# Moving the per-tile VectorE work of a two-layer gated FFN between the blocks of its matmul stream

## The chip, the cores and the metric

The kernel runs on one core of one Trainium2 chip. The metric is the device time in microseconds (us) of one execution. The engines are named as in the profile: PE is TensorE (its weight loads are a separate row, PEld), DVE is VectorE, ACT is ScalarE, POOL is GpSimd, SP is SyncE, which issues most DMAs (114 of the 118 issues in the profile of the kernel before; the other four are POOL's). A run is fast or slow; all comparisons below use fast runs.

## The reference

Two layers, each a gate by a long convolution (A) and a GELU-gated FFN (B), on x of 2048 x 576:

```python
x = A_q
x = x + A(layernorm(x)); x = x + B(layernorm(x))
x = x + A(layernorm(x)); x = x + B(layernorm(x))

# A(q): y depends on k, v and the filters only, not on x
kv = shift_conv(k) * v
y  = irfft(rfft(kv) * rfft(ssm_k)) + kv * ssm_D
A(q) = q * y
# B(x), F = 4608
B(x) = (gelu(x @ w_gate) * (x @ w_up)) @ w_down
```

Because y does not depend on x, it is computed once, at the start.

## The kernel before

The convolution stage fills `y_sb`. Then come eight *units*: layer 0, chunks 0 to 3, then layer 1, chunks 0 to 3. A chunk is 512 rows, which is 4 tiles of 128 rows. A unit goes through 36 *blocks* f of 128 hidden columns. In a block PE does 10 gate/up matmuls (`pg`, `pu`) and 8 down matmuls (`acc`), ACT does the gelu (`ga`), and DVE does `hT = ga * pu`, which the down matmul needs. Between them lies per-tile work on DVE, which below is counted in *pieces*:

```python
def _gate_residual(...):            # one "gate" piece: x + layernorm(x) * y for one tile
    _ln_stats(...)                  # 2 bn_stats, bn_aggr, add eps on DVE; rstd (pow) on POOL
    nc.vector.scalar_tensor_tensor(out=t[:], in0=x_in_ap, scalar=mv[:, 0:1], in1=y_ap, ...)
    nc.vector.scalar_tensor_tensor(out=x_out_ap, in0=t[:], scalar=rstd[:, 0:1], in1=x_in_ap, ...)

def ln_transpose(c):                # for each of 4 tiles one "LN" piece, then the transposes
    for j in range(STC):
        _ln_stats(...)
        nc.vector.tensor_scalar(out=xn[:, 0:D], ...)          # normalised tile, bf16
        # ... 64 more columns of it
    for (c0, dst) in blocks:        # 6 PSUM tiles, 4 transposes each, on PE
        pt = psum_gu.tile([P, CH], BF16, tag="gu")
        # ... 4 x nc.tensor.transpose(pt <- xn)
        nc.vector.tensor_copy(out=dst, in_=pt[:])             # xnT, the rhs of gate/up

def epilogue(layer, c, acc):        # end of a unit
    for j in range(STC):
        # ... x_c (layer 0) or ob (layer 1) <- x_c + acc, two DVE instructions
    for j in range(STC):
        # ... layer 1: DMA out;   layer 0: _gate_residual(...) of the tile, for layer 1
```

The main loop:

```python
psum_gu = ctx.enter_context(tc.tile_pool(name="psum_gu", bufs=3, space=PSUM))
# ... loads of x; gate pieces and ln_transpose of chunk 0
for ui, (layer, c) in enumerate(units):
    # ...
    pgu = gate_up(0)
    for f in range(FT):                                   # FT = 36
        nxt = gate_up(f + 1) if f + 1 < FT else None
        hT = act_mul(*pgu)
        down(f, hT)
        pgu = nxt
        if f == min(6, FT - 1) and ui + 1 < len(units):   # next unit's chunk, in block 6
            nlayer, ncu = units[ui + 1]
            if ncu != c:
                if nlayer == 0:
                    gate_A1(ncu)                          # 4 gate pieces
                nxt_cur = ln_transpose(ncu)               # 4 LN pieces, 24 transposes
    epilogue(layer, c, acc)
```

The instructions of an engine do not run in the order of this text. In the trace of before, the four gates of chunk 1, written in block 6 of unit 0, run from 220.60 to 237.98 us, and the down matmuls of block 1 start only at 238.27. Where two compete, the one written first went first: the gates ahead of hT(0) (348.42 and 356.82 us).

Of the kernel before, what the change touches and what calls it, by code (L numbers as in the profile page):

```python
# [11 lines left out]
ALU = mybir.AluOpType  # L12
F32 = mybir.dt.float32
BF16 = mybir.dt.bfloat16
# [3 lines left out]
P = 128  # L18
# [218 lines left out]
def _ln_stats(nc, small, x_ap, D, eps_t, neghalf_t, mv_out, rstd_out, pfx):  # L237
    nchunk = 2 if D > nc.vector.BN_STATS_FMAX else 1
    w = D // nchunk
    stats = small.tile([P, nchunk, nc.vector.BN_STATS_DIM], F32, tag=pfx + "stats")  # L240
    for h in range(nchunk):
        nc.vector.bn_stats(out=stats[:, h, :], in_=x_ap[:, h * w:(h + 1) * w])  # L242
    nc.vector.bn_aggr(out=mv_out, in_=stats[:])
    ve = small.tile([P, 1], F32, tag=pfx + "ve")
    nc.vector.tensor_scalar_add(out=ve[:], in0=mv_out[:, 1:2], scalar1=eps_t[:, 0:1])  # L245
    nc.gpsimd.tensor_tensor(out=rstd_out, in0=ve[:], in1=neghalf_t[:, 0:1], op=ALU.pow)  # L246


def _gate_residual(nc, small, work, x_in_ap, y_ap, x_out_ap, D, eps_t, neghalf_t):
    mv = small.tile([P, 2], F32, tag="g_mv")  # L250
    rstd = small.tile([P, 1], F32, tag="g_rstd")
    _ln_stats(nc, small, x_in_ap, D, eps_t, neghalf_t, mv[:], rstd[:], "g_")
    t = work.tile([P, D], F32, tag="g_t", bufs=1)
    nc.vector.scalar_tensor_tensor(out=t[:], in0=x_in_ap, scalar=mv[:, 0:1], in1=y_ap,
                                   op0=ALU.subtract, op1=ALU.mult)
    nc.vector.scalar_tensor_tensor(out=x_out_ap, in0=t[:], scalar=rstd[:, 0:1], in1=x_in_ap,  # L256
                                   op0=ALU.mult, op1=ALU.add)
# [3 lines left out]
def ssm_geglu_kernel(ctx, tc, A_q, A_k, A_v, A_shift_k, A_ssm_k, A_ssm_D, B_x, B_w_gate, B_w_up,  # L261
                     B_w_down, out, debug=None):
    nc = tc.nc
    q2 = A_q[0]
    out2 = out[0]
    S, D = q2.shape
# [3 lines left out]
    NCH = S // CH  # L270
    STC = CH // P
    FT = F // P
# [56 lines left out]
    def xs(st):  # L329
        return x_c[st // STC][:, st % STC, :]  # L330

    def gate_A1(c):
        for j in range(STC):
            st = c * STC + j
            _gate_residual(nc, small, work, xs(st), y_sb[:, st, :], xs(st), D, eps_t, neghalf_t)

    psum_gu = ctx.enter_context(tc.tile_pool(name="psum_gu", bufs=3, space=PSUM))
    psum_acc = ctx.enter_context(tc.tile_pool(name="psum_acc", bufs=1, space=PSUM))
# [1 line left out]
    NLAYER = 2  # L340
    units = [(layer, c) for layer in range(NLAYER) for c in range(NCH)]

    def ln_transpose(c):
        xns = []
        for j in range(STC):
            st = c * STC + j
            mv = small.tile([P, 2], F32, tag="mv")
            rstd = small.tile([P, 1], F32, tag="rstd")
            _ln_stats(nc, small, xs(st), D, eps_t, neghalf_t, mv[:], rstd[:], "l_")
            xn = xnp.tile([P, XW], BF16, tag=f"xn{j}", bufs=1)  # L350
            nc.vector.tensor_scalar(out=xn[:, 0:D], in0=xs(st), scalar1=mv[:, 0:1],
                                    scalar2=rstd[:, 0:1], op0=ALU.subtract, op1=ALU.mult)
            if DREM:
                nc.gpsimd.memset(xn[:, D:D + DREM], 0.0)
                nc.vector.tensor_scalar(out=xn[:, D + DREM:XW], in0=xs(st)[:, D - DREM:D],
                                        scalar1=mv[:, 0:1], scalar2=rstd[:, 0:1],
                                        op0=ALU.subtract, op1=ALU.mult)
            xns.append(xn)
        xnT = xnp.tile([P, NDTF, CH], BF16, tag="xnT")
        xnT_rA = xnT_rB = None  # L360
        blocks = [(dt * P, xnT[:, dt, :]) for dt in range(NDTF)]
        if DREM:
            xnT_rA = xnp.tile([P, CH], BF16, tag="xnT_rA", name="xnT_rA")
            xnT_rB = xnp.tile([P, CH], BF16, tag="xnT_rB", name="xnT_rB")
            blocks.append((NDTF * P, xnT_rA[:]))
            blocks.append((NDTF * P + DREM, xnT_rB[:]))
        for (c0, dst) in blocks:
            pt = psum_gu.tile([P, CH], BF16, tag="gu")
            for j in range(STC):
                nc.tensor.transpose(out=pt[:, j * P:(j + 1) * P], in_=xns[j][:, c0:c0 + P], identity=ident[:])  # L370
            nc.vector.tensor_copy(out=dst, in_=pt[:])
        return xnT, xnT_rA, xnT_rB

    def epilogue(layer, c, acc):
        last_layer = layer == NLAYER - 1
        obs = []
        for j in range(STC):
            st = c * STC + j
            if last_layer:
                ob = work.tile([P, D], BF16, tag="pd_bf", bufs=3)  # L380
                obs.append(ob)
                dst_ap = lambda lo, hi: ob[:, lo:hi]
            else:
                dst_ap = lambda lo, hi: xs(st)[:, lo:hi]
            nc.vector.tensor_tensor(out=dst_ap(0, DM), in0=xs(st)[:, 0:DM], in1=acc[:, j, 0:DM], op=ALU.add)  # L385
            if DR:
                nc.vector.tensor_tensor(out=dst_ap(DM, D), in0=xs(st)[:, DM:D],
                                        in1=acc[:, STC, j * DR:(j + 1) * DR], op=ALU.add)
        for j in range(STC):
            st = c * STC + j  # L390
            if last_layer:
                eng = nc.sync
                eng.dma_start(out=out2[st * P:(st + 1) * P, :], in_=obs[j][:])
            else:
                _gate_residual(nc, small, work, xs(st), y_sb[:, st, :], xs(st), D, eps_t, neghalf_t)

    for c in range(NCH):
        nc.gpsimd.dma_start(out=x_c[c][:],
                            in_=q2[c * CH:(c + 1) * CH, :].rearrange("(st p) d -> p st d", p=P))
    gate_A1(0)  # L400
    wpool = ctx.enter_context(tc.tile_pool(name="weights", bufs=1))
    for g in range(1, NFG):
        alloc_w(wpool, g)
        load_w(g)
    cur = ln_transpose(units[0][1])
    for ui, (layer, c) in enumerate(units):
        xnT, xnT_rA, xnT_rB = cur
        acc = psum_acc.tile([P, STC + (1 if DR else 0), 512], F32, tag="acc")

        def gate_up(f):  # L410
            g, fi = divmod(f, FG)
            pg = psum_gu.tile([P, CH], F32, tag="gu")
            pu = psum_gu.tile([P, CH], F32, tag="gu")
            for (pd, wm, rr) in ((pg, wg[g], xnT_rA), (pu, wu[g], xnT_rB)):
                for dt in range(NDTF):
                    nc.tensor.matmul(pd[:], lhsT=wm[:, dt, fi * P:(fi + 1) * P], rhs=xnT[:, dt, :],  # L416
                                     start=(dt == 0), stop=(dt == NDTF - 1 and not DREM))
                if DREM:
                    nc.tensor.matmul(pd[:], lhsT=wr[g][:, fi * P:(fi + 1) * P], rhs=rr[:],  # L419
                                     start=False, stop=True)  # L420
            return pg, pu

        def act_mul(pg, pu):
            ga = work.tile([P, CH], F32, tag="ga")
            nc.scalar.activation(out=ga[:], in_=pg[:], func=ACT.Gelu_apprx_tanh)  # L425
            hT = work.tile([P, CH], BF16, tag="hT", bufs=3)
            nc.vector.tensor_tensor(out=hT[:], in0=ga[:], in1=pu[:], op=ALU.mult)  # L427
            return hT

        def down(f, hT):  # L430
            g, fi = divmod(f, FG)
            for j in range(STC):
                nc.tensor.matmul(acc[:, j, 0:DM], lhsT=hT[:, j * P:(j + 1) * P], rhs=wd[g][:, fi, 0:DM],  # L433
                                 start=(f == 0), stop=(f == FT - 1))
                if DR:
                    nc.tensor.matmul(acc[:, STC, j * DR:(j + 1) * DR], lhsT=hT[:, j * P:(j + 1) * P],  # L436
                                     rhs=wd[g][:, fi, DM:D], start=(f == 0 and j == 0),
                                     stop=(f == FT - 1), skip_group_check=True)

        nxt_cur = None  # L440
        pgu = gate_up(0)
        for f in range(FT):
            nxt = gate_up(f + 1) if f + 1 < FT else None
            hT = act_mul(*pgu)
            down(f, hT)
            pgu = nxt
            if f == min(6, FT - 1) and ui + 1 < len(units):
                nlayer, ncu = units[ui + 1]
                if ncu != c:
                    if nlayer == 0:  # L450
                        gate_A1(ncu)
                    nxt_cur = ln_transpose(ncu)
        epilogue(layer, c, acc)
        if ui + 1 < len(units) and nxt_cur is None:
            if units[ui + 1][0] == 0:
                gate_A1(units[ui + 1][1])
            nxt_cur = ln_transpose(units[ui + 1][1])
        cur = nxt_cur


# [48 lines left out]
```

## Time and profile before

| | before |
|---|---|
| time, median of 4 runs | 1195.13 us (1194.55 to 1195.56) |
| span of the profiled run | 1192.7 us |
| PE busy | 1111.3 us, 93% |
| DVE busy | 489.3 us, 41% |
| FFN stage | from about 230 us to 1186 us |

The head of the page of the kernel before: busy time and share of the span by engine, then PE's busy tenths and the granted PE clock in 40 slices of the span.

```profile
span 1192.7 us, 15798 instructions
...
PE 1111.3 (93%) x6616; PEld 531.0 (45%) x6616; DVE 489.3 (41%) x964; ACT 274.2 (23%) x496; POOL 56.2 (5%) x110
...
PE   5898998699979999799979997999999999999997
...
PEclk9999999899999999899989998999999999999999
```

PE is busy in nearly all of the FFN stage, except for slices that show 7 or 8. The waits view tells what ended PE's idle time there. Its columns are the engine and line, what it waited for, then the total in us, the number of waits and the longest.

```profile
PE acc L433 <- DVE hT L427: 26.6, 4, 6.7
...
PE pt L370 <- DVE xn L351: 10.0, 6, 8.6
```

Four waits of 6.65 us each, 26.6 us in all, are of the down matmul on hT. The other line is mostly one wait of 8.6 us of the first transposes on xn. The timeline of DVE in the kernel before shows the first of the four, between unit 0 and unit 1. Its columns are start, length, engine, line and instruction; brackets give the idle time before it and what ended that.

```profile
345.50 0.69 DVE L385 TENSOR_TENSOR x_c<-x_c,acc 128x512 f32<-128x512 f32 x1 [1.25 <-PE acc L436]
...
348.29 0.21 DVE L387 TENSOR_TENSOR x_c<-x_c,acc 128x64 f32<-128x64 f32 x1
348.42 1.17 DVE L242 BATCH_NORM_STATS2 stats<-x_c 128x6 f32<-128x288 f32 x3
...
351.31 0.82 DVE L256 SCALAR_TENSOR_TENSOR x_c<-t,rstd,x_c 128x576 f32<-128x576 f32 x1
...
356.82 0.64 DVE L427 TENSOR_TENSOR hT<-ga,pu 128x512 bf16<-128x512 f32 x1
```

At 345.5 to 348.4 us DVE does the residual adds of unit 0. It goes straight on to the gates of those tiles (lines 242 to 256). Only at 356.8 does it do hT(0) of unit 1, whose inputs were there by about 347.6. PE over the same time:

```profile
350.48 0.38 PE L419 MATMUL pg<-xnT_rA,wr 128*128 128x512 bf16 x1
357.51 0.61 PE L433 MATMUL acc<-wd,hT 128*128 128x512 bf16 x1 [6.65 <-DVE hT L427]
```

PE had gone ahead with the gate/up matmuls until the three buffers of `psum_gu` were taken (by `pu` of blocks 0 and 1 and `pg` of block 2, the last of which ends at 350.86 us), and then stood for 6.65 us. The down matmul after the wait takes 0.61 us; in the steady part it takes 0.38. A table by stretches of time (busy time of PE, PEld, DVE, ACT and POOL with the number of instructions, then the granted clock, DMA share and GB/s) gives the reason:

```profile
350.86:357.51 6.65, 0.00 (x0) 0.00 (x1) 6.50 (x18) 0.00 (x0) 2.53 (x3) 0.79 0.00 0
357.51:361.54 4.03, 4.03 (x13) 1.52 (x14) 4.03 (x11) 0.60 (x1) 1.18 (x2) 0.50 0.00 0
361.54:364.69 3.15, 3.15 (x19) 1.50 (x18) 3.15 (x8) 0.60 (x1) 1.53 (x2) 1.00 0.02 5
```

For 4.03 us after the wait the granted clock is 0.50. The second loss is at the start of the FFN. The timeline of DVE there, and then of PE:

```profile
214.30 0.58 DVE L351 TENSOR_SCALAR xn<-x_c,mv,rstd 128x576 bf16<-128x576 f32 x1
...
220.60 1.18 DVE L242 BATCH_NORM_STATS2 stats<-x_c 128x6 f32<-128x288 f32 x3 [3.85 <-DMA x_c<-in_A_q_dram]
...
225.17 0.57 DVE L351 TENSOR_SCALAR xn<-x_c,mv,rstd 128x576 bf16<-128x576 f32 x1
```

```profile
216.84 0.33 PE L370 MATMUL pt<-ident,xn 128*128 128x128 bf16 x3 [0.31 <-ACT y_sb L234]
225.80 0.50 PE L370 MATMUL pt<-ident,xn 128*128 128x128 bf16 x3 [8.63 <-DVE xn L351]
...
229.74 1.91 PE L416 MATMUL pg<-xnT,wg 128*128 128x512 bf16 x4
```

DVE's stream has a bn_stats of chunk 1 (at 220.60) ahead of xn of tile 1 of chunk 0 (at 225.17). That bn_stats stood 3.85 us for its DMA, and everything behind it stood too, xn of tiles 1 to 3 among it, whose rstd were done by 217.7 to 218.9 us. After this wait the granted clock of PE was 0.50 from 225.80 to 229.74 us and 0.53 over the next 2.26 us.

To see what each unit boundary costs, I take the time from the gelu of block 30 in one unit to that of block 30 in the next. The second layer's units take 114.49 us: 36 blocks of 3.137 us and 24 transposes (1.55 us), nothing lost. The excess over 114.49 is what a unit boundary and the blocks behind it cost. Before, the first four intervals are 125.25, 125.81, 124.03 and 123.47 us: 40.6 us over.

### The profile page before, as it was taken

The numbers are of one execution on the slowest core, as the hardware profiler recorded it, in microseconds if no ns is written. First come the engines' busy times: TensorE is split into PE (matmuls) and PEld (weight loads), VectorE is DVE, ScalarE is ACT, GpSimd is POOL, SyncE is SP. The second block draws the span as 40 slices with busy tenths as digits, with TensorE's granted clock in tenths as the row PEclk, the third lists the DMA queues.
The fourth block names the chain that finished last, engine by engine and source line by source line (L and its number), as shares of the span: only waits on it lengthen the run. The fifth ranks groups of instructions, "written<-read, shape, count | busy, mean of one in ns | idle before, by whom it ended". The sixth has DMA issues, their size and how long they took to land.

```text
span 1192.7 us, 15798 instructions
## 1 busy us (share of the span) xinstructions
PE 1111.3 (93%) x6616; PEld 531.0 (45%) x6616; DVE 489.3 (41%) x964; ACT 274.2 (23%) x496; POOL 56.2 (5%) x110
## 2 busy tenths in 40 slices
PE   5898998699979999799979997999999999999997
PEld 1443434344434444344434443444444444444443
DVE  5956544842258223962264226422332232223222
ACT  5975222111211121112111121111111111112111
POOL 0001000200012000310010001000000000000000
PEclk9999999899999999899989998999999999999999
DMA  7821000990000000000000000000000000000000
GB/s 238 244 75 40 1 1 1 259 320 17 1 1 1 1 1 1 1 1 1 1 1 1 1 1 1 1 1 2 20 1 1 1 21 1 1 1 20 1 1 20
DMA packets 33654, 38.74 MB, mean 32 GB/s; under 512 B 1845, under 2 KB 31408, under 8 KB 33584
## 3 DMA queue, kind: packets, MB, share of 16 engines
q1 hardware_dynamic: 31472, 33.03, 9.4%
q0 software_dynamic: 2112, 4.72, 1.4%
q8 instruction: 51, 0.84, 0.3%
q14 instruction: 19, 0.16, 0.0%
HBM read 33.02 MB, written 2.36 MB: 30 GB/s over the span
## 4 chain that ended last, share of the span: by engine, by line
PE 84%; DVE 9%; ACT 2%; DMA 2%; issue 2%; POOL 1%; SPq 1%; DVEq 0%; POOLq 0%; ACTq 0%
PE acc L433 20%; PE pu L416 20%; PE pg L416 19%; PE pu L419 5%; PE pg L419 5%; PE ps L231 4%; PE ps L125 3%; PE Yps L219 3%; PE acc L436 3%; DVE stats L242 1%; POOL rstd L246 1%; DVE x_c L256 1%; PE pt L370 1%; DVE x_c L385 1%; DVE pr L216 1%
## 5 line engine op out<-in xcount | busy, mean ns | idle before, releaser
L427 DVE TENSOR_TENSOR hT<-ga,pu 128x512 bf16<-128x512 f32 x288 | 197.6, 686 | 596.7 <-PE pu L419 595.6
L433 PE MATMUL acc<-wd,hT 128*128 128x512 bf16 x1152 | 327.2, 384 | 26.6 <-DVE hT L427 26.6
L425 ACT ACTIVATE ga<-pg 128x512 f32<-128x512 f32 x288 | 172.0, 597 | 778.2 <-PE pg L419 727.5
L416 PE MATMUL pu<-xnT,wu 128*128 128x512 bf16 x1152 | 299.1, 382 | 0.0
L416 PE MATMUL pg<-xnT,wg 128*128 128x512 bf16 x1152 | 296.7, 380 | 0.0
L436 PE MATMUL acc<-wd,hT 128*128 128x64 bf16 x1152 | 223.4, 194 | 0.0
L433 PEld LDWEIGHTS <-hT 128*128 128x128 bf16 x1152 | 113.8, 99 | 166.9 <-DVE hT L427 30.4
L416 PEld LDWEIGHTS <-wu 128*128 128x128 bf16 x1152 | 113.2, 99 | 137.7 <-issue 3.9
L416 PEld LDWEIGHTS <-wg 128*128 128x128 bf16 x1152 | 94.1, 98 | 103.3 <-issue 0.5
L436 PEld LDWEIGHTS <-hT 128*128 128x128 bf16 x1152 | 113.7, 99 | 32.9 <-issue 1.1
L419 PE MATMUL pu<-xnT_rB,wr 128*128 128x512 bf16 x288 | 110.1, 382 | 0.0
L419 PE MATMUL pg<-xnT_rA,wr 128*128 128x512 bf16 x288 | 109.4, 380 | 0.0
L419 PEld LDWEIGHTS <-wr 128*128 128x128 bf16 x576 | 56.6, 98 | 68.7 <-issue 1.4
L216 DVE TENSOR_TENSOR pr<-KVf,Hf 128x2048 bf16<-128x2048 bf16 (+1 forms) x80 | 55.5, 753 | 54.6 <-PE Yps L219 54.5
L246 POOL TENSOR_TENSOR rstd<-ve,neghalf_t 128x1 f32<-128x1 f32 x64 | 46.9, 741 | 541.3 <-DVE ve L245 537.0
L231 PE MATMUL ps<-yb,GI 128*128 128x512 bf16 (+1 forms) x448 | 58.8, 286 | 1.5 <-ACT yb L222 1.3
L125 PEld LDWEIGHTS <-GF 128*128 128x128 bf16 x512 | 34.4, 99 | 52.4 <-issue 15.7
L242 DVE BATCH_NORM_STATS2 stats<-x_c 128x6 f32<-128x288 f32 x128 | 52.7, 433 | 3.8 <-DMA x_c<-in_A_q_dram 3.8
L125 PE MATMUL ps<-hT_blk,GF 128*128 128x512 bf16 (+1 forms) x256 | 38.6, 306 | 13.4 <-ACT GF L59 5.9
L219 PE MATMUL Yps<-pr,ident 128*128 128x512 bf16 (+1 forms) x150 | 38.5, 383 | 10.5 <-ACT yb L222 10.4
L231 PEld LDWEIGHTS <-GI 128*128 128x128 bf16 x448 | 30.1, 98 | 29.4 <-issue 3.1
L125 PE MATMUL ps<-kv_blk,GF 128*128 128x512 bf16 (+1 forms) x256 | 32.8, 286 | 2.1 <-DVE kv_blk L186 1.1
(56 smaller groups left out, 413.7 us busy)
## 6 DMA issues: line engine op xcount, KB each, us to landing
kj<-in_A_k_dram SPq DMA_DIRECT2D x29, 288.0 KB, 3.7
wd<-in_B_w_down_dram SPq DMA_DIRECT2D x9, 576.0 KB, 7.5
wg<-in_B_w_gate_dram SPq DMA_DIRECT2D x9, 512.0 KB, 8.8
wu<-in_B_w_up_dram SPq DMA_DIRECT2D x9, 512.0 KB, 9.7
x_c<-in_A_q_dram POOLq DMA_DIRECT2D x4, 1152.0 KB, 7.8
v_t<-in_A_v_dram SPq DMA_DIRECT2D x8, 288.0 KB, 4.8
out_dram<-ob SPq DMA_DIRECT2D x16, 144.0 KB, 1.8
hn<-in_A_ssm_k_dram SPq DMA_DIRECT2D x4, 512.0 KB, 6.3
```

The lines of the kernel that those rows point to most:

```text
L125: nc.tensor.matmul(ps[:], lhsT=GF[:, kt, mt * P:(mt + 1) * P], rhs=src_blk[:, kt, d0:d0 + dw], start=(kt == 0), stop=(kt == KT_F - 1))
L216: nc.vector.tensor_tensor(out=pr[:], in0=kvp_, in1=hp_, op=ALU.mult)
L219: nc.tensor.matmul(Yflat[:, c0:c0 + cw], lhsT=idm[:], rhs=prf[:, c0:c0 + cw], start=(ti == 0), stop=(ti == n_terms - 1))
L231: nc.tensor.matmul(ps[:], lhsT=GI[:, kt, toff + mt * P: toff + (mt + 1) * P], rhs=ysrc[:, kt, :], start=(i == 0), stop=(i == nmm - 1))
L242: nc.vector.bn_stats(out=stats[:, h, :], in_=x_ap[:, h * w:(h + 1) * w])
L246: nc.gpsimd.tensor_tensor(out=rstd_out, in0=ve[:], in1=neghalf_t[:, 0:1], op=ALU.pow)
L416: nc.tensor.matmul(pd[:], lhsT=wm[:, dt, fi * P:(fi + 1) * P], rhs=xnT[:, dt, :], start=(dt == 0), stop=(dt == NDTF - 1 and not DREM))
L419: nc.tensor.matmul(pd[:], lhsT=wr[g][:, fi * P:(fi + 1) * P], rhs=rr[:], start=False, stop=True)
L425: nc.scalar.activation(out=ga[:], in_=pg[:], func=ACT.Gelu_apprx_tanh)
L427: nc.vector.tensor_tensor(out=hT[:], in0=ga[:], in1=pu[:], op=ALU.mult)
L433: nc.tensor.matmul(acc[:, j, 0:DM], lhsT=hT[:, j * P:(j + 1) * P], rhs=wd[g][:, fi, 0:DM], start=(f == 0), stop=(f == FT - 1))
L436: nc.tensor.matmul(acc[:, STC, j * DR:(j + 1) * DR], lhsT=hT[:, j * P:(j + 1) * P], rhs=wd[g][:, fi, DM:D], start=(f == 0 and j == 0), sto ...
```

## The change

The intent is to take the gate pieces out of the way of hT. Three things move, and no arithmetic is added or removed:

- (a) the four gates after a first-layer unit are kept as `pending` and written one each into blocks 1 to 4 of the next unit;
- (b) gates and LN of the next chunk are written one piece per block from block 6 (or from the first free block), and the transposes after the last of them, in block 10 or 14;
- (c) in unit 0 those pieces get an ordering edge (`issue_after`): on DVE they come only after the last xnT copy of chunk 0.

The output DMAs also move next to their adds. The core of the diff, shortened:

```diff
-    def ln_transpose(c):
+    def ln_begin(c): ...       # state for 4 tiles
+    def ln_st(stt, j): ...     # stats and xn of one tile
+    def ln_finish(stt): ...    # transposes and xnT copies
# ...
-    def epilogue(layer, c, acc):
+    def residual_adds(layer, c, acc):
# ... the adds stay; the gates leave, the DMA is issued beside its add
+        tasks = {}
+        fslot = 1
+        for t in pending:
+            tasks.setdefault(min(fslot, FT - 1), []).append(t)
+            fslot += 1
+        pending = []
# ...
+                nxt_state = ln_begin(ncu)
+                fslot = max(fslot, 6)
+                for j in range(STC):
+                    if nlayer == 0:
+                        tasks.setdefault(min(fslot, FT - 1), []).append(lambda j=j, ncu=ncu: gate_A1_st(ncu * STC + j))
+                        fslot += 1
+                    tasks.setdefault(min(fslot, FT - 1), []).append(lambda j=j, stt=nxt_state: ln_st(stt, j))
+                    fslot += 1
+                tasks.setdefault(min(fslot, FT - 1), []).append("finish")
# ... in the loop over f, in place of the block at f == 6:
+            for t in tasks.get(f, []):
+                if t == "finish":
+                    nxt_cur = ln_finish(nxt_state)
+                elif ui == 0:
+                    with tc.issue_after(first_copy):
+                        t()
+                else:
+                    t()
-        epilogue(layer, c, acc)
+        residual_adds(layer, c, acc)
+        if layer < NLAYER - 1:
+            for j in range(STC):
+                pending.append(lambda j=j, c=c: gate_A1_st(c * STC + j))
```

More of the change, by code (lines that the diff above doesn't have):

```diff
@@ L330, in xs, with gate_A1_st @@
         return x_c[st // STC][:, st % STC, :]
-    def gate_A1(c):
-        for j in range(STC):
-            st = c * STC + j
-            _gate_residual(nc, small, work, xs(st), y_sb[:, st, :], xs(st), D, eps_t, neghalf_t)
+    def gate_A1_st(st):
+        _gate_residual(nc, small, work, xs(st), y_sb[:, st, :], xs(st), D, eps_t, neghalf_t)
     psum_gu = ctx.enter_context(tc.tile_pool(name="psum_gu", bufs=3, space=PSUM))
@@ L341, in ssm_geglu_kernel, with ln_begin, ln_st, ln_finish @@
     units = [(layer, c) for layer in range(NLAYER) for c in range(NCH)]
-    def ln_transpose(c):
-        xns = []
-        for j in range(STC):
-            st = c * STC + j
-            mv = small.tile([P, 2], F32, tag="mv")
-            rstd = small.tile([P, 1], F32, tag="rstd")
-            _ln_stats(nc, small, xs(st), D, eps_t, neghalf_t, mv[:], rstd[:], "l_")
-            xn = xnp.tile([P, XW], BF16, tag=f"xn{j}", bufs=1)
-            nc.vector.tensor_scalar(out=xn[:, 0:D], in0=xs(st), scalar1=mv[:, 0:1],
-                                    scalar2=rstd[:, 0:1], op0=ALU.subtract, op1=ALU.mult)
-            if DREM:
-                nc.gpsimd.memset(xn[:, D:D + DREM], 0.0)
-                nc.vector.tensor_scalar(out=xn[:, D + DREM:XW], in0=xs(st)[:, D - DREM:D],
-                                        scalar1=mv[:, 0:1], scalar2=rstd[:, 0:1],
-                                        op0=ALU.subtract, op1=ALU.mult)
-            xns.append(xn)
+    class LNState:
+        pass
+    def ln_begin(c):
+        stt = LNState()
+        stt.c = c
+        stt.xns = [None] * STC
+        return stt
+    def ln_st(stt, j):
+        st = stt.c * STC + j
+        mv = small.tile([P, 2], F32, tag="mv")
+        rstd = small.tile([P, 1], F32, tag="rstd")
+        _ln_stats(nc, small, xs(st), D, eps_t, neghalf_t, mv[:], rstd[:], "l_")
+        xn = xnp.tile([P, XW], BF16, tag=f"xn{j}", bufs=1)
+        nc.vector.tensor_scalar(out=xn[:, 0:D], in0=xs(st), scalar1=mv[:, 0:1],
+                                scalar2=rstd[:, 0:1], op0=ALU.subtract, op1=ALU.mult)
+        if DREM:
+            nc.gpsimd.memset(xn[:, D:D + DREM], 0.0)
+            nc.vector.tensor_scalar(out=xn[:, D + DREM:XW], in0=xs(st)[:, D - DREM:D],
+                                    scalar1=mv[:, 0:1], scalar2=rstd[:, 0:1],
+                                    op0=ALU.subtract, op1=ALU.mult)
+        stt.xns[j] = xn
+    last_copy = [None]
+    def ln_finish(stt):
+        xns = stt.xns
         xnT = xnp.tile([P, NDTF, CH], BF16, tag="xnT")
@@ L370, in ln_transpose @@
                 nc.tensor.transpose(out=pt[:, j * P:(j + 1) * P], in_=xns[j][:, c0:c0 + P], identity=ident[:])
-            nc.vector.tensor_copy(out=dst, in_=pt[:])
+            last_copy[0] = nc.vector.tensor_copy(out=dst, in_=pt[:])
         return xnT, xnT_rA, xnT_rB
-    def epilogue(layer, c, acc):
+    def residual_adds(layer, c, acc):
         last_layer = layer == NLAYER - 1
-        obs = []
         for j in range(STC):
@@ L380, in epilogue @@
                 ob = work.tile([P, D], BF16, tag="pd_bf", bufs=3)
-                obs.append(ob)
                 dst_ap = lambda lo, hi: ob[:, lo:hi]
@@ L388, in epilogue @@
                                         in1=acc[:, STC, j * DR:(j + 1) * DR], op=ALU.add)
-        for j in range(STC):
-            st = c * STC + j
             if last_layer:
-                eng = nc.sync
-                eng.dma_start(out=out2[st * P:(st + 1) * P, :], in_=obs[j][:])
-            else:
-                _gate_residual(nc, small, work, xs(st), y_sb[:, st, :], xs(st), D, eps_t, neghalf_t)
+                nc.sync.dma_start(out=out2[st * P:(st + 1) * P, :], in_=ob[:])
     for c in range(NCH):
@@ L399, in ssm_geglu_kernel @@
                             in_=q2[c * CH:(c + 1) * CH, :].rearrange("(st p) d -> p st d", p=P))
-    gate_A1(0)
+    for j in range(STC):
+        gate_A1_st(j)
     wpool = ctx.enter_context(tc.tile_pool(name="weights", bufs=1))
@@ L404, in ssm_geglu_kernel @@
         load_w(g)
-    cur = ln_transpose(units[0][1])
+    st0 = ln_begin(units[0][1])
+    for j in range(STC):
+        ln_st(st0, j)
+    cur = ln_finish(st0)
+    first_copy = last_copy[0].ins
+    pending = []
     for ui, (layer, c) in enumerate(units):
@@ L438, in down @@
                                      stop=(f == FT - 1), skip_group_check=True)
+        tasks = {}
[3 more added lines that the diff above has]
+            fslot += 1
+        pending = []
+        nxt_state = None
+        if ui + 1 < len(units):
+            nlayer, ncu = units[ui + 1]
+            assert ncu != c or NCH == 1
+            if ncu != c:
+                nxt_state = ln_begin(ncu)
+                fslot = max(fslot, 6)
+                for j in range(STC):
+                    if nlayer == 0:
[4 more added lines that the diff above has]
+                tasks.setdefault(min(fslot, FT - 1), []).append("finish")
         nxt_cur = None
@@ L446, in ssm_geglu_kernel @@
             pgu = nxt
-            if f == min(6, FT - 1) and ui + 1 < len(units):
-                nlayer, ncu = units[ui + 1]
-                if ncu != c:
-                    if nlayer == 0:
-                        gate_A1(ncu)
-                    nxt_cur = ln_transpose(ncu)
-        epilogue(layer, c, acc)
-        if ui + 1 < len(units) and nxt_cur is None:
-            if units[ui + 1][0] == 0:
-                gate_A1(units[ui + 1][1])
-            nxt_cur = ln_transpose(units[ui + 1][1])
+            for t in tasks.get(f, []):
[8 more added lines that the diff above has]
+        if layer < NLAYER - 1:
+            for j in range(STC):
+                pending.append(lambda j=j, c=c: gate_A1_st(c * STC + j))
+        if ui + 1 < len(units) and nxt_cur is None:
+            for t in pending:
+                t()
+            pending = []
+            stn = ln_begin(units[ui + 1][1])
+            for j in range(STC):
+                ln_st(stn, j)
+            nxt_cur = ln_finish(stn)
         cur = nxt_cur
```

## The prediction

> **What bounds the kernel now.** The FFN stage (230 to 1186 us) is TensorE-bound: the page has PE 93% busy, the chain of waits is 84% PE. In the timeline one hidden block f repeats every 3.137 us. Second-layer units start their first down matmul 114.48 us apart: 36 x 3.137 plus 24 transposes (1.55), nothing lost. First-layer intervals are 122.38, 125.25, 125.81, 124.03, then 115.58: 40.7 us over 5 x 114.48.
>
> Cause, in the waits view: four times "PE acc <- DVE hT", 6.65 us each. The timeline at 345 to 358 us shows DVE running 4 residual adds (2.9 us), nearly all four gate_residuals (about 2.1 us each, rstd on POOL between), and only then hT(0) of the next unit, at 356.8, though its inputs are ready by 347.6. PE gets 5.6 us ahead, fills the three gate/up PSUM buffers and stops. Afterwards the granted clock is 0.50 for 4.0 us (matmuls 0.61 instead of 0.38 us): another 2 us each. [...] The rest, 1 to 2 us per unit, is lost near f=6 (378 to 383 us), where gates, LN and transposes of the next chunk crowd hT.
>
> Second loss, the FFN's start: PE idles 217.2 to 225.8 (8.63 us, "pt <- DVE xn"). DVE's in-order stream has bn_stats of chunk 1, whose DMA lands at 220.6, ahead of xn of tiles 1 to 3 of chunk 0, whose rstd are done by 217.7 to 218.9. PE then starts cold.
>
> **The change.** No arithmetic is added or removed. It moves (a) gate_residuals out of the epilogue, one each into blocks f=1..4 of the next unit, behind hT(0), hT(1); (b) gates and LN of the next chunk, one piece per block from f=6, then the transposes; (c) in unit 0 these wait for the last xnT copy; (d) output DMAs beside their adds (0 to 0.4 us).
>
> **Cost.** DVE's steady load is 0.69 of each 3.14 us, so one gate or LN (2.1 us) per block fits; hT has about 1.2 us of slack, more than one filler instruction (0.82 us at most). At 843 to 848 us the trace already has a boundary with residual adds but no gates, and PE does not stop. So
> - boundary stalls gone: 4 x 6.65 = 26.6
> - their cold clocks gone: 4 x 2 = 8
> - crowding at f=6: about 6 at most, half of it gone
> - start: xn1..3 at about 218 to 220 instead of 225 to 227.5, first gate matmul at about 222 instead of 229.7, warm: 8 to 9.
>
> The ceiling is 40.7 + 8.8 = 49.5, giving 1145.6. I leave about 4 us for fillers delaying hT: **1150 us**, range 1144 to 1165. Weights have slack: group 1 should land by 229 and is needed by 234. Chances: faster by over 2% 0.95, within 2% 0.045, slower 0.005.
>
> **What would show it.** Right: no 6.65 us wait of down on hT; first-down intervals 114.5 to 116; clock 1.00 through the FFN; PE's wait for xn at 217 us down to 1 to 2 us; PE about 96% busy; DVE busy unchanged near 489 us. Wrong: new PE waits on hT in blocks 1 to 13, DVE waiting for POOL rstd in front of hT, PE waiting for weight DMAs near 234 us.
>
> **What would make it wrong.** [...] if it places two or three fillers before an hT, each such block loses up to 1 us, and 13 blocks in four units could give back 10 to 20 us. The start could stay late if something else holds it, such as POOL being held by DMA issue (214.7 to 217.0).

The sum came to 40.7 + 8.8 = 49.5 us, less about 4 us for fillers. In the last paragraph, "it" is the order of DVE's instructions in the built program. The slack of hT is read at the boundary at 843 to 848 us, where hT(0) ends at 846.98 and its down matmul starts at 848.18 us. That group 1 of the weights lands by 229 us and is needed by 234 is an estimate that the trace of before bears out: its issues start at 216.7 to 219.0 us, their kind lands after 6.8 to 9.7 us in the median, and four blocks of 3.137 us lie between the expected 222 us and its first use.

## The result, and the profile after

The changed kernel takes 1147.74 us (median of 8 runs, 1146.41 to 1151.23), the kernel before 1194.87 us in the same rounds. The ratio is 0.9609, with a 95% interval of 0.9599 to 0.9619. Ratios here are the mean time of one kernel's fast runs over that of the other's of the same rounds, so they are not quite the ratio of the medians that are quoted. A second measurement of the changed kernel on another occasion gave 1147.88 us and 0.9607.

The head of the page, and the waits, of the changed kernel:

```profile
span 1148.8 us, 15802 instructions
...
PE 1103.2 (96%) x6616; PEld 528.2 (46%) x6616; DVE 487.8 (42%) x964; ACT 274.2 (24%) x496; POOL 54.0 (5%) x110
```

```profile
PE pt L380 <- DVE xn L356: 1.9, 3, 1.2
...
PE acc L442 <- DVE hT L436: 1.0, 3, 0.4
```

PE is busy 96% of a shorter span, and DVE's busy time is what it was (487.8 us). The four waits of 6.65 us are gone; three short ones, 1.0 us together, are left. The boundary between units 0 and 1 on DVE in the changed kernel:

```profile
340.16 0.69 DVE L393 TENSOR_TENSOR x_c<-x_c,acc 128x512 f32<-128x512 f32 x1 [1.25 <-PE acc L445]
...
343.08 0.68 DVE L436 TENSOR_TENSOR hT<-ga,pu 128x512 bf16<-128x512 f32 x1
343.68 0.81 DVE L242 BATCH_NORM_STATS2 stats<-x_c 128x6 f32<-128x288 f32 x2
344.55 0.69 DVE L436 TENSOR_TENSOR hT<-ga,pu 128x512 bf16<-128x512 f32 x1
```

hT(0) now follows the residual adds at once (343.08), hT(1) comes at 344.55, and the gates fill the time between and behind. PE:

```profile
343.19 1.03 PE L425 MATMUL pu<-xnT,wu 128*128 128x512 bf16 x4
344.06 0.38 PE L428 MATMUL pu<-xnT_rB,wr 128*128 128x512 bf16 x1
344.27 0.38 PE L442 MATMUL acc<-wd,hT 128*128 128x512 bf16 x1
```

PE goes from the up matmul to the down matmul without a gap, and the down matmul takes 0.38 us. The start of the FFN in the changed kernel, DVE and then PE:

```profile
216.55 0.58 DVE L356 TENSOR_SCALAR xn<-x_c,mv,rstd 128x576 bf16<-128x576 f32 x1
...
219.97 0.58 DVE L356 TENSOR_SCALAR xn<-x_c,mv,rstd 128x576 bf16<-128x576 f32 x1 [0.96 <-POOL rstd L246]
...
224.37 0.81 DVE L242 BATCH_NORM_STATS2 stats<-x_c 128x6 f32<-128x288 f32 x2
```

```profile
219.10 0.33 PE L380 MATMUL pt<-ident,xn 128*128 128x128 bf16 x3 [0.31 <-ACT y_sb L234]
220.60 0.34 PE L380 MATMUL pt<-ident,xn 128*128 128x128 bf16 x3 [1.18 <-DVE xn L356]
...
223.84 1.87 PE L425 MATMUL pg<-xnT,wg 128*128 128x512 bf16 x4
```

The statistics of chunk 1 (224.37) now come behind xn of all four tiles. The convolution stage of this profiled run ended 2.25 us later than before: the last four evictions of y (ScalarE's copies of y out of PSUM into `y_sb`) start at 217.77 us, against 215.52 us before. From that mark the first gate matmul comes after 6.07 us instead of 14.22, and the first gelu after 9.73 instead of 17.89, so the start gained 8.16 us up to the first gelu. PE's wait for xn is 1.9 us in all.

One thing did not come out as hoped. Stretches of the changed kernel:

```profile
223.84:227.40 3.56, 3.56 (x10) 1.23 (x9) 3.40 (x11) 1.19 (x1) 1.55 (x5) 0.53 1.38 381
227.40:231.00 3.60, 3.60 (x22) 1.68 (x21) 2.36 (x4) 1.29 (x3) 0.00 (x0) 1.00 1.21 366
```

The granted clock is 1.00 at the boundaries (a table below shows it for the first), but still 0.53 in the first 3.6 us of the FFN. That is so in this profile and not in the other one of the same kernel (after_again, below): there PE has the same waits at the start, the clock stays 1.00 (220.73 to 225.00 us), and the first gelu comes 8.68 us after the mark and not 9.73. The half clock at the start was thus not the same in two executions of one kernel. Nine profiles have the early xn. The clock at the start was read in four of them: 1.00 in after_again, 0.53 over 3.56 us here, 0.57 over 4.00 us in paced2 and 0.54 over 2.79 us in late_loads. ScalarE's wait for the first gate result is 6.1 us in after_again's profile and 6.9 to 7.4 us in the other eight.

The account for this profile is 38.5 us from the intervals (40.6 us of excess before, 2.1 us after) and 8.16 us from the start, less 0.56 us that the slow first matmuls cost between the first gelu and that of block 30 (93.88 us, 93.32 before): 46.1 us. The spans differ by 43.9 us, and the later end of the convolution stage (2.25 us) is the rest. In after_again's profile the start gained 9.21 us with nothing lost behind it, 47.7 us in all. The medians differ by 47.1 us.

### The profile page after: what moved, and what is told of

It reads as the page before. It is cut to its first block, busy times and chain, and to the rows that moved or that the text cites. A ratio compares the mean times of both kernels' runs of the same rounds, so it can differ in the third digit from the quotient of the medians.

```text
span 1148.8 us, 15802 instructions
## 1 busy us (share of the span) xinstructions
PE 1103.2 (96%) x6616; PEld 528.2 (46%) x6616; DVE 487.8 (42%) x964; ACT 274.2 (24%) x496; POOL 54.0 (5%) x110
## 4 chain that ended last, share of the span: by engine, by line
PE 85%; DVE 8%; ACT 2%; DMA 2%; issue 1%; POOL 1%; SPq 1%; DVEq 0%; POOLq 0%; ACTq 0%
PE acc L442 20%; PE pg L425 20%; PE pu L425 20%; PE pg L428 5%; PE pu L428 5%; PE ps L231 4%; PE ps L125 3%; PE Yps L219 3%; PE acc L445 3%; DVE x_c L256 1%; DVE stats L242 1%; DVE hT L436 1%; PE pt L380 1%; DVE t L254 1%; DMA kj<-in_A_k_dram 1%
## 5 line engine op out<-in xcount | busy, mean ns | idle before, releaser
L442 PE MATMUL acc<-wd,hT 128*128 128x512 bf16 x1152 | 322.1, 380 | 1.1 <-DVE hT L436 1.0
L125 PE MATMUL ps<-hT_blk,GF 128*128 128x512 bf16 (+1 forms) x256 | 40.7, 317 | 13.6 <-ACT GF L59 6.0
```

What stands on the lines that cost most here:

```text
L125: nc.tensor.matmul(ps[:], lhsT=GF[:, kt, mt * P:(mt + 1) * P], rhs=src_blk[:, kt, d0:d0 + dw], start=(kt == 0), stop=(kt == KT_F - 1))
L442: nc.tensor.matmul(acc[:, j, 0:DM], lhsT=hT[:, j * P:(j + 1) * P], rhs=wd[g][:, fi, 0:DM], start=(f == 0), stop=(f == FT - 1))
```

## The experiments

Excess over 114.49 us in the first four intervals, in us (profiles are of fast runs unless noted):

| kernel | parts | 0 to 1 | 1 to 2 | 2 to 3 | 3 to 4 | time, us | ratio to before |
|---|---|---|---|---|---|---|---|
| before | none | 10.8 | 11.3 | 9.5 | 9.0 | 1195 | 1 |
| after (run again) | a, b, c | 0.7 | 1.4 | 0.0 | 0.0 | 1147.88 | 0.9607 |
| c_start_only | c | 10.8 | 11.3 | 9.6 | 9.0 | 1186.61 | 0.9926 |
| b_spread_only | b | 8.8 | 9.2 | 8.2 | 8.3 | 1188.69 | 0.9951 |
| a_gates_only | a | slow profile | – | – | – | 1180.29 | 0.9868 |
| no_spread | a, c | 11.7 | 11.7 | 0.0 | 0.0 | 1168.78 | 0.9787 |
| no_issue_after | a, b | 0.7 | 1.3 | 0.0 | 0.0 | 1158.65 | 0.9681 |
| bunch_late_T | a, c, late transposes | 10.1 | 9.3 | 0.0 | 0.0 | 1164.08 | 0.9738 |
| burst_f1 | a in one block, b, c | 2.8 | 2.5 | 2.0 | 2.0 | 1154.95 | 0.9662 |
| keep_warm | none, dummy matmuls | 11.1 | 11.6 | 7.3 | 7.3 | 1190.69 | 0.9969 |
| paced2 | a, b with edges, c | 0.0 | 0.0 | 0.0 | 0.0 | 1145.43 | 0.9584 |
| best2 | paced2 and late loads | 0.0 | 0.0 | 0.0 | 0.0 | 1146.74 | 0.9594 |

The theory at the outset was that of the prediction: each part removes its own loss. The rivals are in the expectations.

### after_again: the changed kernel once more

It ran unchanged, on the same chip as no_spread, bunch_late_T and paced2, so that these can be compared with it directly.

> The changed kernel once more, on this chip, as the mark for the other runs of this call: 1146 to 1149 us, ratio 0.961.

Measured: 1147.88 us, ratio 0.9607 (0.9586 to 0.9629), as expected. Its profile is of a faster execution (span 1144.1 us against 1148.8): the convolution stage ended 3.1 us earlier, and the FFN began at the full clock.

### c_start_only: part (c) alone

```diff
 # the kernel before
                     if nlayer == 0:
-                        gate_A1(ncu)
+                        if ui == 0:
+                            with tc.issue_after(first_copy):   # last xnT copy of chunk 0
+                                gate_A1(ncu)
+                        else:
+                            gate_A1(ncu)
```

> The kernel before with part (c) alone: in unit 0 the next chunk's gates are issued on DVE only after the last xnT copy. My theory (DVE's in-order stream waited for the DMA of chunk 1): the 8.63 us PE wait for xn becomes 1 to 2 us in all, the first gate matmul comes 7.6 us earlier relative to the end of the convolution stage, the four boundary stalls of 6.65 us stay; 1187 to 1188 us, ratio about 0.9935. Rival (POOL, held by issuing the loads, or the loads themselves set the start): ratio 0.998 or more.

Measured: 1186.61 us, ratio 0.9926 (0.9906 to 0.9946). The waits of 6.65 us stayed, 26.6 us in all. The start is that of the changed kernel: in this kernel PE waits 1.18, 0.37 and 0.37 us for xn. The theory holds: the bn_stats that stood for its DMA ahead of xn on DVE was what held the start (PE's longest wait for xn was 8.63 us before).

### no_issue_after: part (c) undone in the changed kernel

```diff
-                elif ui == 0:
-                    with tc.issue_after(first_copy):
-                        t()
                 else:
                     t()
```

> The changed kernel without the ordering edge of unit 0 (part c undone, all else kept). My theory: DVE again has bn_stats of chunk 1 ahead of xn of tiles 1 to 3, PE waits about 8.6 us for xn once, boundaries stay clean; 1155 to 1156 us, ratio about 0.967. Rival (ranking the next chunk's pieces at block 6 and later already keeps them out of the start): 1148 us, ratio 0.961.

Measured: 1158.65 us (1154.64 to 1160.00), ratio 0.9681 (0.9654 to 0.9709), some 3 us above the expected time, which lies within the spread of its runs. The times of the four runs follow their mean granted clock (0.994 at 1154.64 us, 0.987 at 1160.00 us), so a lower clock is at least a part of the 3 us. In the waits view of this kernel the old wait is back, and the boundaries stay clean:

```profile
PE pt L380 <- DVE xn L356: 9.0, 3, 8.6
...
PE acc L442 <- DVE hT L436: 0.9, 3, 0.4
```

So writing the pieces of chunk 1 into block 6 and later does not keep them out of the start; the edge does. Part (c) is worth 8.8 us by the ratios in both directions (0.9926 alone; 0.9681 against 0.9607); by the medians it is 8.6 and 10.8 us.

### a_gates_only: part (a) alone

```diff
 # the kernel before
             else:
-                _gate_residual(nc, small, work, xs(st), y_sb[:, st, :], xs(st), D, eps_t, neghalf_t)
+                pending.append(st)
 # ... and in the loop over f
             pgu = nxt
+            if f >= 1 and pending:
+                st = pending.pop(0)
+                _gate_residual(nc, small, work, xs(st), y_sb[:, st, :], xs(st), D, eps_t, neghalf_t)
```

> The kernel before with part (a) alone: the four gate_residuals of a first-layer unit leave the epilogue and are issued one each in blocks 1 to 4 of the next unit. My theory (the boundary stalls are an ordering matter on DVE and hold 34 us of stall and cold clock): the four 6.65 us waits of the down matmul on hT vanish, first-down intervals fall to 114.5 to 117 us, the clock stays 1.00 there, the 8.6 us PE wait for xn at the FFN start stays; time 1156 to 1162 us, ratio about 0.967 to 0.972. Rival (DVE has too much work around the boundary whatever the order, and the gain needs the spreading of the next chunk's LN and gates too): intervals stay above 119 us and the ratio above 0.98.

Measured: 1180.29 us, ratio 0.9868 (0.9843 to 0.9893). **The expectation failed**: 15 us came, not 34 to 39. Its profile only gave a hint. The boundary waits were gone in it, but PE now waited for xn in block 6 of units 1 and 2, 8.0 us each. That led to a new theory, tested with the next three kernels.

Theory A. What is written ahead of hT(f) and is not done yet delays hT(f), so it has to fit into DVE's spare time before f. DVE's steady load is one hT of 0.69 us per block of 3.137 us, so the spare time is about 2.45 us per block. A gate or an LN piece takes about 2.1 us. Both are estimates from the trace of before. Before, the 4 gates of the epilogue had no block at all ahead of hT(0), and the 8 pieces of block 6 (17 us) had about seven blocks (17 us). With part (a) alone units 1 and 2 have 12 pieces ahead of hT(7), 25 us, and still about 17 us of spare time. 8 us are missing.

### no_spread: part (b) undone in the changed kernel

```diff
-                        tasks.setdefault(min(fslot, FT - 1), []).append(lambda j=j, ncu=ncu: gate_A1_st(ncu * STC + j))
-                        fslot += 1
-                    tasks.setdefault(min(fslot, FT - 1), []).append(lambda j=j, stt=nxt_state: ln_st(stt, j))
-                    fslot += 1
+                        tasks.setdefault(6, []).append(lambda j=j, ncu=ncu: gate_A1_st(ncu * STC + j))
+                for j in range(STC):
+                    tasks.setdefault(6, []).append(lambda j=j, stt=nxt_state: ln_st(stt, j))
+                fslot = 6                                  # transposes in block 6 too
```

> The changed kernel with part (b) undone: all gates and LN of the next chunk and the transposes again in block 6, parts (a) and (c) kept. Theory A, formed from the kernel with part (a) alone: what ranks ahead of hT(f) must fit into DVE's spare time before f, about 2.45 us per block (3.137 less 0.69). Units 1 and 2 then have 12 pieces of about 2.1 us, 25 us, ranked ahead of hT(7) with 7 x 2.45 = 17 us to do them in, so PE stands about 8 us in block 6 to 7 of these two units and restarts on the half clock (2 us); 20 us over the changed kernel, 1165 to 1172 us, ratio 0.975 to 0.981. Theory B (my blind prediction: at block 6 only a few us of crowding are at stake, and part (b) is worth about 3 us): 1151 us, ratio 0.963.

Measured: 1168.78 us, ratio 0.9787 (0.9764 to 0.9810), as Theory A says. Two hT in a row on DVE in this kernel, and what PE did:

```profile
356.42 0.68 DVE L436 TENSOR_TENSOR hT<-ga,pu 128x512 bf16<-128x512 f32 x1
357.01 0.81 DVE L256 SCALAR_TENSOR_TENSOR x_c<-t,rstd,x_c 128x576 f32<-128x576 f32 x1
...
364.42 0.58 DVE L356 TENSOR_SCALAR xn<-x_c,mv,rstd 128x576 bf16<-128x576 f32 x1 [0.30 <-POOL rstd L246]
...
369.30 0.63 DVE L436 TENSOR_TENSOR hT<-ga,pu 128x512 bf16<-128x512 f32 x1
```

```profile
365.06 0.40 PE L380 MATMUL pt<-ident,xn 128*128 128x128 bf16 x2 [5.51 <-DVE xn L356]
367.07 0.40 PE L380 MATMUL pt<-ident,xn 128*128 128x128 bf16 x2 [1.62 <-DVE xn L356]
369.10 0.39 PE L380 MATMUL pt<-ident,xn 128*128 128x128 bf16 x2 [1.62 <-DVE xn L356]
...
370.76 0.61 PE L442 MATMUL acc<-wd,hT 128*128 128x512 bf16 x1
```

Between the hT at 356.42 and the next at 369.30 lie 12.9 us, filled with gates and LN but for three waits of 0.30 us for rstd. PE waits 5.51 + 1.62 + 1.62 us at the transposes and then runs at 0.61 us per matmul. So without part (b) the gain of part (a) is paid back a few blocks later, in the two units that have both sets of gates.

### bunch_late_T: the pieces bunched, the transposes late

As no_spread, but with `fslot = 14` for the transposes. It asks whether PE's stall comes from the transposes that stand ahead of the gate/up matmuls before their xn are ready, or from hT(7) behind the pieces on DVE.

> As no_spread, all gates and LN of the next chunk in block 6, but the transposes after block 14. [...] Theory A (hT starved): PE waits on hT instead of xn in block 6 to 7 of units 1 and 2, and the time is within 3 us of no_spread, 1163 to 1172 us. Theory C (the early transposes are what blocks PE): no stall, 1147 to 1150 us.

Measured: 1164.08 us, ratio 0.9738 (0.9720 to 0.9756), 4.7 us below no_spread and within the expected range of times, if a little more than the 3 us. The one PE wait at the same place is now on hT:

```profile
370.84 0.61 PE L442 MATMUL acc<-wd,hT 128*128 128x512 bf16 x1 [7.20 <-DVE hT L436]
```

In no_spread PE stops at the transposes after the down matmul of 359.13 us; here PE still runs 15 gate/up matmuls, a block and a half (360.24 to 363.64 us), before it stops. But taking the transposes out of the way does not free PE here: the same DVE backlog then shows as 7.20 us on hT. The early transposes are a few us of the loss, not its cause; Theory C falls.

### b_spread_only: part (b) alone

The changed kernel with the gates called at once after the residual adds, in place of `pending.append`, and without the edge of unit 0.

> The kernel before with part (b) alone: the gates stay in the epilogue and nothing is held back at the start, only the next chunk's gates, LN and transposes are spread over blocks 6 to 14. It measures what (b) is worth by itself; after (a) it is worth about 20 us (no_spread against the changed kernel). Theory A (the work ranked ahead of hT(7) is only short of time when part (a) has put four gates more into the blocks before it): the four boundary waits of 6.65 us stay, the 4.0 us of crowding at block 6 of units 1 and 2 go, 1191 to 1192 us, ratio 0.996 to 0.998. Rival (b is worth about 20 us wherever it is applied): 1175 us, ratio 0.983.

Measured: 1188.69 us, ratio 0.9951 (0.9939 to 0.9963), 6.3 us off. The four waits of 6.65 us stay (26.6 us). Of the intervals' 6.2 us, 4.1 us are in the first two, where the crowding was. The other two gave 1.4 and 0.7 us, which I had not expected: fewer matmuls ran at half clock after those waits (at the third boundary a clock of 0.51 for 2.9 us, where before there were 4.03 us at 0.50 and 1.60 us more at 0.52). Part (b) removes nothing there, so these 2.1 us are not shown to be its own. By the medians part (b) alone is so worth 6.3 us, and after (a) and (c) it is worth 20.9 us (no_spread less the changed kernel). The parts do not add.

### burst_f1: the four deferred gates in one block

```diff
-            tasks.setdefault(min(fslot, FT - 1), []).append(t)
-            fslot += 1
+            tasks.setdefault(1, []).append(t)
+        fslot = 1 + len(pending)
         pending = []
```

> The changed kernel with all four deferred gates issued together in block 1 instead of one each in blocks 1 to 4. hT(0) and hT(1) still rank ahead of them, hT(2) does not. My theory (what counts is how many hT rank behind about 8.4 us of gates that become ready only after the residual adds): a new stall of PE on hT(2), 3 to 5 us at each of the four first-layer boundaries, intervals 118 to 121 us; 1160 to 1172 us, ratio 0.971 to 0.981. Rival (it is enough that hT(0) and hT(1) go first, since PE has two blocks queued): no new wait, 1147 to 1149 us, ratio 0.961.

Measured: 1154.95 us, ratio 0.9662 (0.9643 to 0.9681). The direction is that of my theory, but the stall is 1.79 us at each of the four boundaries and not 3 to 5. The waits view has these four and one of 0.46 us:

```profile
PE acc L442 <- DVE hT L436: 7.6, 5, 1.8
```

The sum fits the time: 4 x 1.79 = 7.2 us over 1147.74. Two blocks of lead absorb most of the four gates, not all. These waits did not lower the clock (1.00 in the 3.3 to 3.9 us after each). The same burst written into block 6 was built as well; I found the same order of instructions as in the changed kernel, so it was not run. What part (a) needs is enough hT written ahead of the gates; that they need not be one per block is not shown by a run.

### keep_warm: the stall kept, PE kept busy

```diff
 # the kernel before; the columns written are read by nobody
             hT = act_mul(*pgu)
+            if f == 0 and 1 <= ui <= 4:
+                for _ in range(60):
+                    nc.tensor.matmul(acc[:, STC, 256:512], lhsT=ident[:], rhs=xnT[:, 0, 0:256],
+                                     start=True, stop=True, skip_group_check=True)
             down(f, hT)
```

> The kernel before, with 60 dummy matmuls (128x256, into columns of the accumulator's fifth bank that nothing reads) on PE before the first down matmul of units 1 to 4, so that PE has work during the stall; the stall itself, set by hT(0), stays. They take about 6.5 us of the 7.8 us before hT(0) comes. If the half clock after the stall comes from PE's idleness, matmuls after the boundary take 0.38 instead of 0.61 us, the granted clock is 1.00 there, and the 0.90 + 1.42 + 1.65 + 1.09 us now lost in the first two blocks after the four boundaries are saved: about 1190 us, ratio 0.995 to 0.997. If the low clock has another cause, or the dummies delay the down matmul, the ratio is 1.000 or more.

Measured: 1190.69 us, ratio 0.9969 (0.9951 to 0.9988). PE at the first boundary of this kernel:

```profile
348.19 6.71 PE L447 MATMUL acc<-xnT,ident 128*128 128x256 bf16 x60
...
356.08 0.39 PE L433 MATMUL acc<-wd,hT 128*128 128x512 bf16 x1 [0.54 <-DVE hT L427]
```

The dummies take 6.71 us (the expected 6.5 us agree with an estimate from the trace: a block's matmuls read 7424 columns in 3.137 us, the dummies 15360), and the down matmul behind them takes 0.39 us, not 0.61; the clock stays 1.00 over the 4.0 to 4.1 us measured at each of the four boundaries, where it was 0.50 over 4.0 us in the kernel before. So at these boundaries the half clock does come from PE's idleness and costs time by itself. It is also a second case of a gain paid back. The third and fourth intervals lost 2.3 and 1.7 us less than before, but the first two did not: in units 1 and 2 PE now waits 1.79 us for xn in block 6 where it waited 0.26 us. My reading, not tested, is that blocks that run faster leave DVE less time before block 6. In unit 1 the clock did not fall after this wait (down matmuls of 0.38 us from 378.61 us on); in unit 2 it fell:

```profile
503.15 0.40 PE L370 MATMUL pt<-ident,xn 128*128 128x128 bf16 x4 [1.79 <-DVE xn L351]
504.31 0.63 PE L433 MATMUL acc<-wd,hT 128*128 128x512 bf16 x1
```

From 503.15 to 507.00 us the granted clock was 0.56. So a wait of 1.79 us was followed by the half clock here and not in burst_f1 (1.00).

### paced2: the pieces held back to their blocks

The changed kernel still lost 2.1 us in blocks 8 to 11 of units 1 and 2. There DVE runs almost without a break for 39 us (its waits for rstd are 0.66 us at most), because pieces are taken as early as they are ready, ahead of their block.

```diff
 # the changed kernel
-            fslot += 1            # three places
+            fslot += 2
-                elif ui == 0:
-                    with tc.issue_after(first_copy):
-                        t()
                 else:
-                    t()
+                    with tc.issue_after(last_hT[0].ins):      # hT of this block
+                        t()
```

> The changed kernel with each deferred piece tied on DVE behind the hT of its own block by an ordering edge, and one piece every second block (4 gates in blocks 1, 3, 5, 7, the next 8 pieces from 9 on, transposes after the last). The changed kernel still loses 2.1 us in blocks 8 to 11 of units 1 and 2, where DVE is fully busy for 39 us from the boundary on, because pieces are taken as early as they are ready. Theory A: with the pieces held back no hT is late, all first-down intervals are 114.5 us, and the time is about 2 us below the changed kernel, 1145 to 1146 us. Rival (an isolated piece exposes DVE to the wait for POOL's rstd, about 1 us each, and delays the hT behind it): intervals of 115 us or more and no gain.

Measured: 1145.43 us, ratio 0.9584 (0.9565 to 0.9603), with 1147.88 us for the changed kernel on the same chip. The two intervals of the ratios overlap, so the gain in time is not settled; the trace shows that the lost 2.1 us are gone: all intervals are 114.48 or 114.49 us, and PE has no wait on hT at all. DVE's load at the first boundary, first of the changed kernel, then of this one:

```profile
339.90:379.80 39.90, 39.49 (x223) 18.26 (x222) 36.75 (x92) 7.76 (x13) 8.58 (x12) 1.00 0.00 1
```

```profile
334.00:374.00 40.00, 39.79 (x226) 18.85 (x228) 25.87 (x56) 7.76 (x13) 5.14 (x6) 1.00 0.00 1
```

36.75 us busy of 39.9 became 25.87 us of 40.0. The stretches are of equal length and the work was moved behind them, not removed. The rival cost, DVE waiting for POOL's rstd (xn waits 20.4 us for it in all, where it waited 4.5 us), did not reach PE.

### late_loads and best2: the rest of the start

```diff
 # the changed kernel: loads of x chunks 1 to 3 written after the LN pieces of chunk 0
-    for c in range(NCH):
-        # ... load of chunk c
+    load_x(0)
     # ... gate and LN pieces of chunk 0
+    for c in range(1, NCH):
+        load_x(c)
```

> The changed kernel with the loads of x chunks 1 to 3 traced after the LN of chunk 0. At the start xn of tile 1 now waits 0.96 us for rstd, because POOL issues these three loads for 2.27 us first. Theory (POOL's DMA issue holds the start by one to two us): xn of tile 1 starts about 2 us earlier, that of tile 3 1 to 1.5 us earlier, first gate matmul likewise; 1146 to 1147 us, ratio 0.9595 to 0.960. Rival (the last tile's statistics, done at 218.8, set the start): no change, ratio 0.961.

Measured: 1149.59 us, ratio 0.9612 (0.9599 to 0.9625): no gain. From the last evictions of y the first gate matmul came after 5.96 us against 6.07 us. xn of tile 1 did start early, but tile 2 waited for its statistics and rstd as before. The rival holds.

> paced2 and late_loads together: 2.1 us from the pacing and 1 to 1.5 us from the start, 1144 to 1145 us, ratio 0.957 to 0.958.

Measured: 1146.74 us, ratio 0.9594 (0.9580 to 0.9609). It keeps the clean intervals of paced2 and gains nothing from the loads, so paced2 has the lowest median of all that was run. Both are under the changed kernel by less than their intervals resolve.

## Why the prediction was right, and where not

The time (1150 us predicted, 1147.74 us measured, range 1144 to 1165) and the cause of the gain held. Point by point:

- *Boundary stalls, 4 x 6.65 = 26.6 us.* Gone, as shown by the waits view. The wait came from the order on DVE, shown by burst_f1, where moving only the gates' place brought a wait back.
- *Cold clocks, 4 x 2 = 8 us.* That they come from PE's wait is shown by keep_warm (0.50 after the waits, 1.00 after the same waits filled). The size was a little low. In the traces of before, the first blocks after the four boundaries take 0.90, 1.42, 1.65 and 1.09 us too long, although 1.08 us of their gate matmuls had been done ahead: 9.4 us in all.
- *Crowding at f=6, about 6 at most, half of it gone.* The loss behind the boundaries of units 1 and 2 was 4.0 us before and is 2.1 us after. But the reading of part (b) behind this line was wrong. I wrote it as a loss of its own, worth about 3 us, beside the others. It is the condition under which (a) pays: (a) alone brought 15 us, (a) with (c) left 21 us on the table, and (b) alone brought 6 us. The argument that "one gate or LN (2.1 us) per block fits" was right and should have been turned round: eight of them written in block 6 behind four deferred ones do not fit. Had the change lacked (b), a sum of terms like mine would have promised about 1152 us, and 1168.78 us was measured. That this error did not show in the time is luck: the change contained (b).
- *Start, 8 to 9 us, "warm".* 8.16 us to the first gelu in one profile and 9.21 in the other; c_start_only and no_issue_after show the cause. "Warm" came true in after_again's profile (1.00) and not in the three others in which the clock was read there: it was 0.53 for the first 3.6 us in the changed kernel's first profile, with the same waits on PE as in after_again's, 0.57 in paced2 and 0.54 in late_loads. The earlier xn alone brings the first gate matmul forward by 8.15 us in both.
- *About 4 us for fillers delaying hT.* 2.1 us were measured, in blocks 8 to 11 of units 1 and 2; paced2 shows that they were that. They are the same 2.1 us as under crowding, counted once.
- *Clock 1.00 through the FFN.* True from 227.4 us on, false for the start in that profile; true for all of it in after_again's. First-down intervals of 114.48 to 115.83 us, PE at 96% and DVE's unchanged busy time came as written.

The output DMAs' move was not tried by itself; the tail from the start of the last matmul on is 6.8 us before and after, so it is within 0.1 us here.

What carries the argument about the waits is the traces' own order and durations: in before a bn_stats stood 3.85 us for a DMA on DVE and xn of tiles whose rstd were done by 217.7 to 218.9 us came behind it, at 225.17 us and later; with the edge PE's longest wait for xn fell from 8.63 to 1.18 us. The half clock behind the waits is a cost of its own.

## What to carry to other kernels

When work on a side engine is put off to free the critical one, add up all that is then written ahead of each instruction the critical engine waits for, and compare it with the side engine's spare time up to that point; an average load of 41% said nothing about that here. Parts of such a change need not add (here 14.9, 6.3 and 8.6 us alone, 47.1 us together): measure each one undone as well as alone, for a gain can be paid back a few blocks later at the next place where work is bunched. Where instructions run ahead of their place in the text, as here, a later place may not hold them back: in no_issue_after PE waited 8.6 us for xn with the pieces written in block 6 and later, and with an explicit ordering edge its longest wait was 1.2 us.

## What the runs show of the half clock

- Gaps and the clock. After PE's gaps of 6.65 us in before the granted clock was 0.50 for 4.0 us. After the four of 1.79 us in burst_f1 it was 1.00; of two such gaps in keep_warm, one was followed by a clock of 0.56 over 3.85 us. At the FFN's start of the changed kernel the longest gap was 1.18 us in both profiles, and in the first of them PE was busy 0.33 to 0.50 us in each of the 4 us from 219 us on; the clock fell to 0.53 in one and stayed 1.00 in the other. Why equal gaps ended differently is not shown.
- A trial of filling a wait with matmuls: 60 dummy matmuls at each of four waits took 3.4 us off the four intervals (4.7 us off the median, ratio 0.9969), less than the 9.4 us lost at half clock. Part was paid back on DVE, as the intervals show; that the dummies also displaced matmuls done ahead is my guess for the rest.
- What deferred work has to fit into: here pieces of 2.1 us against 2.45 us of spare time per block decided over about 21 us (no_spread less the changed kernel).
